# Reordered first loads, a smaller constant, and the second pair turned later, in a state-space kernel with a bilinear feed-forward layer

## The chip, the cores and the metric

The kernel runs on one core of one Trainium2 chip. The core has a matrix engine (TensorE, PE in the profile), three engines for elementwise work (VectorE or DVE, ScalarE or ACT, GpSimd or POOL), and a queue engine for transfers (SyncE or SP). SP, ScalarE and GpSimd can each issue transfers. The metric is the device time of one launch in microseconds, the median of three runs: before the change 125.71 us (125.55 to 125.74).

## The reference

Inputs are x (4 batches, 8 heads, 768 steps, 32 wide), a decay a per step, B and C (16 wide), and three weights of the feed-forward layer. The first stage is a chunked scan, the second a bilinear layer without a nonlinearity:

```python
for c in range(nc):                      # chunks of 32 steps, per batch and head
    cum = np.cumsum(log_a_chunk, axis=-1)
    L = np.exp(cum[..., :, None] - cum[..., None, :]) * causal
    y_intra = (C @ B.T * L) @ x
    y_inter = (C @ state) * np.exp(cum)[..., None]
    y[chunk] = y_intra + y_inter
    state = exp(sum(la)) * state + sum_j(B_j x_j exp(cum[-1] - cum_j))
x2 = y.transpose(0, 2, 1, 3).reshape(3072, 256)
out = ((x2 @ w_a) * (x2 @ w_b)) @ w_out  # w_a, w_b: 256 x 1536; w_out: 1536 x 256
```

## The kernel before

The kernel uses chunks of 128 steps (six blocks of the 768) and works on pairs of batches: pair 0 is block 0 of batches 0 and 1, pair 1 is block 0 of batches 2 and 3, pair 2 begins block 1, and so on to pair 11. For a pair it does the following.

- *Factors.* VectorE scans the products of a (`scan`, L236), takes reciprocals at the middle of a block (`over_mid`, L240), and scales a selector by them (`sel_over_mid`, L243). Eight small TensorE products for a block (`factors_mm`, L251) turn this into factors per step and head, in PSUM. ScalarE copies them to fC, and VectorE writes their reciprocals to fB.
- *Scaled B and C.* `scale_bc` (L310) multiplies B by fB into `bm` and C by fC into `cm`, for pair 0 on VectorE and for pairs 1, 2 and 3 on GpSimd.
- *Turns.* `transposes` (L326) turns bm and cm on TensorE (`turn`), copies the turned B twice into BT with two masks of rows (`copy_bt`), and copies the turned C into CT.
- *Scores, masks, outputs.* `scores` (L378) makes C times B in four PSUM banks SC, `mask` (L431) multiplies by the causal mask on VectorE, or by way of ScalarE on GpSimd, and `pv_u` (L440) multiplies by x, which `scale_x` (L297) has scaled to 16 bit. The result is evacuated into X2T.
- *Feed-forward.* `units_mm` (L637) and `unit` (L622 and L662) make products of X2T with Wa and Wb into banks `aps` and `bps`. ScalarE copies aps to `asb` (`evac_a`, L649), VectorE multiplies it with bps into hk (`times`, L654), and products with Wo give the output.

The order of the work is written out by hand: each engine executes its instructions in the order of the program, and waits at an instruction until its inputs are there. Every call of `bank` (L132) takes the next digit of the string BANKS as its PSUM bank, so the same string also decides which earlier work a TensorE group waits for.

The loads are issued in program order on their queues as well. SP loads a, parts of pair 0's inputs and the constants `ch` and `c32` (L182 to L194). ScalarE loads the other parts of pair 0 and then its activation table (L192). GpSimd loads pair 1's B and C, the first half of Wa in two pieces, the first piece of the first half of Wb, and pair 1's x (L219 to L227). It then scales pair 1's B and C, and only after that issues the second piece of Wb's first half and the second halves of Wa and Wb (L798 to L802). Later on its queue come pair 2's inputs and the two halves of Wo (L842 to L848). A transfer on GpSimd's queue also waits until the one eight places before it on that queue has landed, because eight completion counters are used in turn: the second half of Wo waits in this way for the second half of Wb. Pair 3's inputs go by SP and are held back by a dependency on the second half of Wb (L873, L874).

Before and between the early steps TensorE executes products on zeros (`warmup`, L229), whose results nobody reads.

Of the kernel before, what the change touches and what calls it, by code (L numbers as in the profile page):

```python
# [10 lines left out]
f32 = mybir.dt.float32  # L11
# [10 lines left out]
BANKS = (  # L22
    "0123120321032101320132013203120132013201321031230123012310321032130213021031203120321301"
    "2031203120312302130213021302103210321032103210321032103210231023102310231023102310231023"
    "102310231"
)
# [3 lines left out]
def kernel(  # L30
# [13 lines left out]
    nc = tc.nc  # L44
# [17 lines left out]
    bh = np.arange(BH)  # L62
    p32 = np.zeros((128, 128 + nb * NG), np.float32)
    p32[0:BH, 0:128] = (bh[:, None] % H) == (j[None, :] // N)
    for b in range(nb):
# [7 lines left out]
    const = ctx.enter_context(tc.tile_pool(name="const", bufs=1))  # L73
    c32 = const.tile([128, p32.shape[1]], f32, name="c32")
    ch = const.tile([128, H + 2], f32, name="ch")
# [69 lines left out]
    def load1(eng, p, which, bt, i0=0, n=64):  # L145
        blk, bp = divmod(p, NBP)
        if p >= P0:
            return eng.dma_start(
                by_token(pair_in[p][which])[:, bt],
                (B, C, x)[which][2 * bp + bt, :, blk * Q : (blk + 1) * Q, :].rearrange("h q n -> q h n"),  # L150
            )
        src = (B, C, x)[which][2 * bp + bt, :, blk * Q + 2 * i0 : blk * Q + 2 * i0 + 2 * n, :]
        return eng.dma_start(  # L153
            pair_in[p][which][64 * bt + i0 : 64 * bt + i0 + n].rearrange("i h r n -> i h (r n)"),
            src.rearrange("h (i r) n -> i h (r n)", r=2),
        )
# [19 lines left out]
    def load_wo(half):  # L176
        nc.gpsimd.dma_start(
            Wo[:, 6 * half : 6 * half + 6].rearrange("p (g kk) e -> p g (kk e)", kk=3),
            moe_w_out.rearrange("(g p kk) e -> p g (kk e)", p=128, kk=3)[:, 2 * half : 2 * half + 2],
        )  # L180

    nc.sync.dma_start(a_sb, a.rearrange("b h (k q) -> (b h) k q", q=Q))  # L182
    for p_ in range(3):
# [6 lines left out]
    load1(nc.scalar, 0, 1, 0, 32, 32)  # L190
    load1(nc.scalar, 0, 2, 1)
    nc.scalar.preload_act_table_set("natural_log_exp_and_others")  # L192
    load1(nc.sync, 0, 2, 0)
    nc.sync.dma_start(c32, p32_t.ap())  # L194
    nc.vector.memset(sel, 1.0)
# [4 lines left out]
    nc.vector.memset(hsx, 0.0)  # L200
    nc.vector.memset(causal_q, 1.0)
    nc.gpsimd.affine_select(
        out=sel,
# [10 lines left out]
    for bt in range(2):  # L214
# [3 lines left out]
        )  # L218
    load1(nc.gpsimd, 1, 0, 0)  # L219
    load1(nc.gpsimd, 1, 0, 1)  # L220
    load1(nc.gpsimd, 1, 1, 0)
    load1(nc.gpsimd, 1, 1, 1)
    load_w(Wa, 0, 0)
    load_w(Wa, 0, 1)
    load_w(Wb, 0, 0)
    for bt in range(2):
        load1(nc.gpsimd, 1, 2, bt)  # L227

# [97 lines left out]
    def transposes(p, ps=None, between=None, apart=False, tb2=None):  # L326
        s = st[p]
        if p >= P0:
            ps = [bank("tr").bitcast(f16)] * 2
            TB, TC = ps[0][:, 0:256], ps[0][:, 256:512]  # L330
            on_dve = False
        elif ps is None:
            ps = [SC[0], bank("tc") if p == 1 else SC[1]] if apart else None
            on_dve = apart
            TB, TC = (TT[:, 0:256], TT[:, 256:512]) if ps is None else [t_.bitcast(f16)[:, 0:256] for t_ in ps]
        else:
            on_dve = False
            TB, TC = [t_.bitcast(f16)[:, 0:256] for t_ in ps]
# [8 lines left out]
        def copy_bt(e):  # L347
            o_ = BT[:, e].rearrange("p r t i -> p (r t i)")
            if p == 0 and e:
                nc.vector.tensor_scalar(o_, tb2, par[:, e : e + 1], None, ALU.mult)  # L350
            else:
                b_.append(nc.scalar.activation(out=o_, in_=TB, func=AF.Copy, scale=par[:, e : e + 1]))  # L352

        turn(TB, s["bm"])
        if p == 1:
            copy_bt(0)
            copy_bt(1)
        if between:
            between()
        turn(TC, s["cm"])  # L360
        if p == 0:
            turn(tb2, s["bm"])
        if p != 1:
            copy_bt(0)
            copy_bt(1)
        if p >= P0:
# [4 lines left out]
            CT.rearrange("p t (i r) -> p r (t i)", r=2), TC.rearrange("p (r c) -> p r c", r=2)  # L371
        )
        if apart:
            for i_ in b_:
                tc.declare_no_dep(c_.ins, i_.ins.name, reason="reads of two banks")
# [401 lines left out]
    vr, fr = [t_.rearrange("p (r b h) -> p r b h", r=2, b=NBP) for t_ in (v, flat(fB, 0, 1))]  # L777
    nc.vector.reciprocal(fr[:, :, 0], vr[:, :, 0])
    warmup(2, SC[3])
# [5 lines left out]
    nc.vector.reciprocal(fr[:, :, 1], vr[:, :, 1])  # L785
    nc.scalar.copy(flat(fC, 0, 1), v)
    over_mid(1, 2)
    warmup(1, SC[3])
    warmup(2, SC[3], 128)
    scores(0)  # L790
    mask(product0(0, 0))
    mask(product0(0, 1))
    scale_x(0, nc.scalar)
    for e in range(2):
        mask(product0(1, e))
    warmup(2, tcp)
    warmup(2, tcp)
    scale_bc(1, 0, nc.gpsimd)  # L798
    scale_bc(1, 1, nc.gpsimd)
    load_w(Wb, 0, 1)  # L800
    load_w(Wa, 1)
    w1 = [load_w(Wb, 1)]  # L802
    sel_over_mid(1, 2, nc.gpsimd)
    nc.gpsimd.affine_select(
        out=causal_q, in_=causal_q, compare_op=ALU.is_ge, fill=0.0, base=0, pattern=[[1, Q]], channel_multiplier=-1
    )
    py = [bank("py0"), bank("py1")]
# [34 lines left out]
    for w in range(2):  # L842
        for bt in range(2):
            load1(nc.gpsimd, 2, w, bt)
    load_wo(0)
# [12 lines left out]
    nc.scalar.copy(maskbd, headm.unsqueeze(2).broadcast_to((128, H, D)))  # L858
# [242 lines left out]
```

## Time and profile before

| | us |
|---|---|
| median of three runs | 125.71 |
| the profiled execution | 125.44 |
| its span in the profile | 123.7 |
| TensorE busy (share of the span) | 117.1 (95%) |
| VectorE busy | 90.3 (73%) |
| ScalarE busy | 75.6 (61%) |
| GpSimd busy | 62.1 (50%) |

The profile is one execution. Its span is measured from the first to the last instruction that it shows, and the rest of its time lies around that. TensorE was granted its full clock in the whole span. A row of the timeline gives the start in us from the beginning of the span, the length in us, the engine, the line of the kernel, the operation, what it wrote and read, how many instructions are grouped, and in brackets how long the engine had been idle before and what ended that idle time. A row with SPq, ACTq or POOL and DMA_DIRECT2D is the issue of a transfer and not the transfer. A row of issues gives the size of one transfer and the median time from issue to landing.

### The profile page before, as it was taken

The page shows a single profiled execution, that of the slowest core. Times are in us where ns is not written, and L with a number is a line of the kernel's source. Part 1 is how long each engine was busy: PE and PEld are TensorE (multiplying, and loading weights), DVE is VectorE, ACT ScalarE, POOL GpSimd, SP SyncE. Part 2 cuts the span into 40 slices and gives each one's busy share as a digit, 9 for nine tenths or more (in the row PEclk, how much of TensorE's full clock was granted, in tenths as well). Part 3 has the DMA queues.
Part 4 walks back from the last instruction along what each step waited for, and adds up shares of the span by engine and source line. Part 5 has one row for each costly group of instructions (what it writes and reads, how often), then busy time and mean ns, then how long its engine had stood idle before and what let it go on. Part 6 is the DMA issues. An engine that isn't in the chain of part 4 may idle for free.

```text
span 123.7 us, 3723 instructions
## 1 busy us (share of the span) xinstructions
PE 117.1 (95%) x1467; PEld 80.7 (65%) x1467; DVE 90.3 (73%) x179; ACT 75.6 (61%) x158; POOL 62.1 (50%) x90
## 2 busy tenths in 40 slices
PE   5979799999999999999999999999999999999990
PEld 1436588889898798744467465757464775555890
DVE  3777898872995979799986988996889444747200
ACT  0447756827759856987669767457637746657220
POOL 6999996599392995097997970056000000000000
PEclk9999999999999999999999999999999999999999
DMA  3999999989999998689958921011101012010122
GB/s 65 160 184 205 156 213 212 168 154 91 99 117 129 89 123 109 70 109 102 89 171 182 276 56 45 5 42 45 42 0 48 0 42 87 5 42 0 42 85 85
DMA packets 56001, 12.21 MB, mean 99 GB/s; under 512 B 50640, under 2 KB 55504, under 8 KB 55984
## 3 DMA queue, kind: packets, MB, share of 16 engines
q1 hardware_dynamic: 51632, 7.42, 37.2%
q0 software_dynamic: 2352, 4.20, 18.8%
q10 hardware_dynamic: 2000, 0.36, 1.6%
q8 instruction: 11, 0.18, 0.6%
q14 instruction: 6, 0.05, 0.2%
HBM read 11.19 MB, written 3.15 MB: 116 GB/s over the span
## 4 chain that ended last, share of the span: by engine, by line
PE 79%; POOL 9%; DMA 7%; DVE 2%; issue 1%; ACT 0%; POOLq 0%
PE ops L730 17%; PE aps L705 17%; PE bps L705 16%; PE ops L673 9%; DMA Wb<-in_moe_w_b_dram 7%; PE aps L627 6%; PE bps L627 5%; PE SC L384 2%; PE SC L444 2%; PE tr L345 2%; POOL Wa L170 1%; POOL bn L153 1%; POOL cn L153 1%; POOL xn L153 1%; POOL cm L319 1%
## 5 line engine op out<-in xcount | busy, mean ns | idle before, releaser
L651 ACT COPY asb<-aps 128x512 f32<-128x512 f32 x72 | 42.0, 586 | 14.9 <-PE aps L705 10.3
L715 DVE TENSOR_TENSOR hkb<-bps,asb 128x512 f16<-128x512 f32 x48 | 32.4, 688 | 11.7 <-ACT asb L651 10.8
L705 PE MATMUL aps<-XB,Wa 128*128 128x512 f16 x96 | 28.6, 379 | 0.1
L705 PE MATMUL bps<-XB,Wb 128*128 128x512 f16 x96 | 28.5, 379 | 0.0
L730 PE MATMUL ops<-Wo,hkb 128*128 128x256 f16 (+1 forms) x204 | 22.8, 267 | 0.0
L730 PEld LDWEIGHTS <-hkb 128*128 128x128 f16 x204 | 18.5, 98 | 3.0
L438 DVE TENSOR_TENSOR t<-SC,causal_q 128x512 f16<-128x512 f32 x27 | 17.3, 681 | 2.2 <-PE SC L384 2.2
L658 DVE TENSOR_TENSOR hk<-bps,asb 128x512 f16<-128x512 f32 x24 | 15.7, 684 | 3.1 <-ACT asb L651 2.7
L705 PEld LDWEIGHTS <-Wb 128*128 128x128 f16 x96 | 9.9, 103 | 10.9
L705 PEld LDWEIGHTS <-Wa 128*128 128x128 f16 x96 | 9.7, 103 | 9.2 <-issue 0.3
L742 ACT ACTIVATE osb<-ops 128x256 f32<-128x256 f32 (+1 forms) x16 | 6.0, 376 | 12.7 <-PE ops L730 12.6
L627 PE MATMUL aps<-X2T,Wa 128*128 128x256 f16 x88 | 13.1, 273 | 0.0
L627 PE MATMUL bps<-X2T,Wb 128*128 128x256 f16 x84 | 12.5, 273 | 0.0
L308 POOL TENSOR_SCALAR x<-xn 128x512 f16<-128x512 f32 x8 | 11.9, 1489 | 0.8 <-DMA xn<-in_x_dram 0.2
L673 PE MATMUL ops<-Wo,hk 128*128 128x256 f16 x96 | 11.7, 273 | 0.0
L673 PEld LDWEIGHTS <-hk 128*128 128x128 f16 x96 | 9.0, 98 | 1.2
L627 PEld LDWEIGHTS <-Wa 128*128 128x128 f16 x88 | 8.8, 104 | 0.9 <-issue 0.2
L627 PEld LDWEIGHTS <-Wb 128*128 128x128 f16 x84 | 8.5, 103 | 0.6
L436 POOL TENSOR_TENSOR t<-tmp,causal_q 128x512 f16<-128x512 f32 x5 | 5.8, 1155 | 6.2 <-ACT tmp L435 6.1
L438 DVE TENSOR_TENSOR t<-SC,causal 128x512 f16<-128x512 f32 x13 | 8.2, 679 | 0.6 <-PE SC L399 0.6
L607 POOL TENSOR_TENSOR spair<-U,ch 128x128 f16<-128x128 f32 x8 | 3.1, 398 | 10.2 <-DVE U L591 10.2
L352 ACT ACTIVATE bt<-tr,ch 128x256 f16<-128x256 f16 x16 | 6.7, 472 | 0.5 <-PE tr L345 0.5
(105 smaller groups left out, 136.9 us busy)
## 6 DMA issues: line engine op xcount, KB each, us to landing
out_dram<-osb SPq DMA_DIRECT2D x23, 128.0 KB, 1.7
xn<-in_x_dram SPq DMA_DIRECT2D x5, 256.0 KB, 4.9
cn<-in_C_dram SPq DMA_DIRECT2D x8, 128.0 KB, 4.6
bn<-in_B_dram SPq DMA_DIRECT2D x8, 128.0 KB, 4.3
Wo<-in_moe_w_out_dram POOLq DMA_DIRECT2D x2, 384.0 KB, 6.2
xn<-in_x_dram POOLq DMA_DIRECT2D x3, 256.0 KB, 6.6
xn<-in_x_dram POOLq DMA_DIRECT2D x4, 128.0 KB, 5.5
xn<-in_x_dram SPq DMA_DIRECT2D x3, 128.0 KB, 4.9
```

The lines of the kernel that those rows point to most:

```text
L308: eng.tensor_scalar(xo, xi, XS, None, ALU.mult)
L352: b_.append(nc.scalar.activation(out=o_, in_=TB, func=AF.Copy, scale=par[:, e : e + 1]))
L436: nc.gpsimd.tensor_tensor(out=o_, in0=tmp, in1=c_, op=ALU.mult)
L438: nc.vector.tensor_tensor(out=o_, in0=i_, in1=c_, op=ALU.mult)
L627: nc.tensor.matmul(ps[:, kk * 2 * Q : (kk + 1) * 2 * Q], w_up(W, k, f), X2T[:, p, :, f], start=(f == 0), stop=(f == 1), skip_group_check=True,
L651: (nc.vector.tensor_copy if on_dve else nc.scalar.copy)(asb, a_ps)
L658: nc.vector.tensor_tensor(out=s["hk"][:, 2 * k2 : 2 * k2 + 2, :].rearrange("p k q -> p (k q)"), in0=b_ps, in1=asb, op=ALU.mult)
L673: nc.tensor.matmul(o_ps[:, 0:d_model], hk[:, k, bt * Q : (bt + 1) * Q], Wo[:, k, :], start=(k == 0), stop=(k == NK - 1), skip_group_check= ...
L705: nc.tensor.matmul(t_, w_up(W, k, f), XB[:, blk - P0 // NBP, f].rearrange("p t j q -> p (t j q)"), start=(f == 0), stop=(f == 1), skip_gro ...
L715: return lambda: nc.vector.tensor_tensor(out=s["hk"][:, k], in0=ps[1], in1=asb, op=ALU.mult)
L730: nc.tensor.matmul(o_ps[:, 0:w], hk[:, k, c * Q : (c + 1) * Q], Wo[:, k, cs], start=(k == 0), stop=(k == NK - 1), skip_group_check=True,)
L742: nc.scalar.activation(out=o_sb[:, 0:w], in_=o_ps[:, 0:w], func=AF.Copy, scale=1.0 / (YS * YS))
```

## The change

- GpSimd issues the second piece of Wb's first half right after one x transfer of pair 1, ahead of scaling pair 1's B and C.
- The other half of pair 1's x goes by SP. A dependency puts it behind the first reciprocal of factor 0.
- Pair 0's first half of x, one transfer on SP before, is split in two of 32 rows: one on SP, and one on ScalarE's queue ahead of the activation table.
- The constant c32 is loaded with 32 rows of 592 bytes instead of 128, and VectorE writes zeros to the tile first. The load moves behind the x transfer on SP.
- The factor products of block 1 move from behind the first Wb products to right behind pair 0's scores, into the bank that block 0's factors are in. One copy now takes both blocks' factors to fC. The scaling of the selector for block 1 moves from GpSimd to VectorE.
- Pair 1's turns: B is turned into a bank and C into SC[1] (before: SC[0] and a bank). The turn of C no longer comes after pair 0's second output products but before them. Of the two copies of the turned B, ScalarE makes the first and VectorE the second, after its copy of C.
- Pair 1's scores come behind six products with Wa. Three units' products with Wa are all issued early, and of the first products with Wb the last two come behind pair 1's outputs. ScalarE takes all four evacuations of pair 0's outputs.
- Pair 3's inputs are held back by the first half of Wo instead of the second half of Wb.
- BANKS is a new string for the new order.

```diff
-    p32 = np.zeros((128, 128 + nb * NG), np.float32)
+    p32 = np.zeros((BH, 128 + nb * NG), np.float32)
...
+    load1(nc.sync, 0, 2, 0, 0, 32)
+    load1(nc.scalar, 0, 2, 0, 32, 32)
     nc.scalar.preload_act_table_set("natural_log_exp_and_others")
-    load1(nc.sync, 0, 2, 0)
-    nc.sync.dma_start(c32, p32_t.ap())
...
+    nc.vector.memset(c32, 0.0)
+    x1 = load1(nc.sync, 1, 2, 0)
+    nc.sync.dma_start(c32[0:BH], p32_t.ap())
...
     load_w(Wb, 0, 0)
-    for bt in range(2):
-        load1(nc.gpsimd, 1, 2, bt)
+    load1(nc.gpsimd, 1, 2, 1)
+    load_w(Wb, 0, 1)
...
-            ps = [SC[0], bank("tc") if p == 1 else SC[1]] if apart else None
+            ps = [bank("tb") if p == 1 else SC[0], SC[1]] if apart else None
...
-            if p == 0 and e:
-                nc.vector.tensor_scalar(o_, tb2, par[:, e : e + 1], None, ALU.mult)
+            if p < 2 and e:
+                nc.vector.tensor_scalar(o_, tb2 if p == 0 else TB, par[:, e : e + 1], None, ALU.mult)
...
         turn(TB, s["bm"])
-        if p == 1:
-            copy_bt(0)
-            copy_bt(1)
...
         turn(TC, s["cm"])
         if p == 0:
             turn(tb2, s["bm"])
+        copy_bt(0)
         if p != 1:
-            copy_bt(0)
             copy_bt(1)
...
+        if p == 1:
+            copy_bt(1)
...
-    nc.vector.reciprocal(fr[:, :, 0], vr[:, :, 0])
+    f0 = nc.vector.reciprocal(fr[:, :, 0], vr[:, :, 0])
+    tc.add_manual_dep(x1.ins, f0.ins.name, AFTER, reason="x of pair 1 behind x of pair 0")
...
-    nc.scalar.copy(flat(fC, 0, 1), v)
     over_mid(1, 2)
+    sel_over_mid(1, 2, nc.vector)
...
     scores(0)
+    factors_mm(1, 2, fps0, 1)
     mask(product0(0, 0))
     mask(product0(0, 1))
+    scale_bc(1, 0, nc.gpsimd)
+    nc.scalar.copy(flat(fC, 0, 2), fps0[:, 0:64])
     scale_x(0, nc.scalar)
...
-    warmup(2, tcp)
-    warmup(2, tcp)
-    scale_bc(1, 0, nc.gpsimd)
     scale_bc(1, 1, nc.gpsimd)
-    load_w(Wb, 0, 1)
     load_w(Wa, 1)
-    w1 = [load_w(Wb, 1)]
-    sel_over_mid(1, 2, nc.gpsimd)
+    load_w(Wb, 1)
...
+    warmup(4, tb2)
...
-    def second():
-        pv_u(0, 1, py, True)
-        for bt in range(2):
-            evac0(1, bt, (nc.scalar, nc.vector)[bt], py)
-
-    transposes(1, between=second, apart=True)
+    transposes(1, apart=True)
+    pv_u(0, 1, py, True)
+    for bt in range(2):
+        evac0(1, bt, nc.scalar, py)
     scan(3, 5)
-    aps = [bank("aps") for _ in range(2)]
-    units_mm(0, (0, 1), Wa, aps, 0, range(4))
-    units_mm(0, (0, 1), Wa, aps, 1, range(2))
+    aps = [bank("aps") for _ in range(3)]
+    units_mm(0, range(3), Wa, aps, 0, range(6))
+    scores(1)
+    mask(product(1, 3), by_pool=True)
+    units_mm(0, range(3), Wa, aps, 1, range(6))
     asb = [evac_a(aps[0])]
-    scores(1)
-    units_mm(0, (0, 1), Wa, aps, 1, range(2, 4))
-    mask(product(1, 3), by_pool=True)
-    aps.append(unit_mm(0, 2, Wa))
-    asb.append(evac_a(aps[1]))
     scale_x(1, nc.scalar)
-    asb.append(evac_a(aps[2]))
+    asb += [evac_a(aps[1]), evac_a(aps[2])]
...
+    tiles(3)
     bps = [bank("bps") for _ in range(3)]
-    units_mm(0, range(3), Wb, bps, 0, range(6))
-    tiles(3)
+    units_mm(0, range(3), Wb, bps, 0, range(4))
     pv(1, DS=(0, SC[:2]))
     ds_mm(0, 64, SC[:2])
+    units_mm(0, range(3), Wb, bps, 0, range(4, 6))
     units_mm(0, range(3), Wb, bps, 1, range(6))
-    fps = bank("fps")
-    factors_mm(1, 2, fps)
-    nc.scalar.copy(flat(fC, 1, 2), fps[:, 0:32])
...
-    tc.add_manual_dep(b3[0].ins, w1[0].ins.name, AFTER, reason="weights ahead of pair 3's inputs")
+    tc.add_manual_dep(b3[0].ins, wo0.ins.name, AFTER, reason="weights ahead of pair 3's inputs")
```

More of the change, by code (lines that the diff above doesn't have):

```diff
@@ L22 @@
 BANKS = (
-    "0123120321032101320132013203120132013201321031230123012310321032130213021031203120321301"
-    "2031203120312302130213021302103210321032103210321032103210231023102310231023102310231023"
-    "102310231"
+    "0123130213021302312031203102312031203120321023012301230210321032013201321023102310320123"
+    "1023102310230132013201320132103210321032103210321032103213021302130213021302130213021302"
+    "13021302"
 )
@@ L62 @@
     bh = np.arange(BH)
-    p32 = np.zeros((128, 128 + nb * NG), np.float32)
-    p32[0:BH, 0:128] = (bh[:, None] % H) == (j[None, :] // N)
+    p32 = np.zeros((BH, 128 + nb * NG), np.float32)
+    p32[:, 0:128] = (bh[:, None] % H) == (j[None, :] // N)
     for b in range(nb):
@@ L73 @@
     const = ctx.enter_context(tc.tile_pool(name="const", bufs=1))
-    c32 = const.tile([128, p32.shape[1]], f32, name="c32")
+    c32 = const.tile([128, 128 + nb * NG], f32, name="c32")
     ch = const.tile([128, H + 2], f32, name="ch")
@@ L176, in load_wo @@
     def load_wo(half):
-        nc.gpsimd.dma_start(
+        return nc.gpsimd.dma_start(
             Wo[:, 6 * half : 6 * half + 6].rearrange("p (g kk) e -> p g (kk e)", kk=3),
@@ L218 @@
         )
[L219 to L222, printed above, removed]
+    for w in range(2):
+        for bt in range(2):
+            load1(nc.gpsimd, 1, w, bt)
     load_w(Wa, 0, 0)
@@ L790 @@
     scores(0)
+    factors_mm(1, 2, fps0, 1)
     mask(product0(0, 0))
     mask(product0(0, 1))
+    scale_bc(1, 0, nc.gpsimd)
+    nc.scalar.copy(flat(fC, 0, 2), fps0[:, 0:64])
     scale_x(0, nc.scalar)
-    for e in range(2):
-        mask(product0(1, e))
-    warmup(2, tcp)
-    warmup(2, tcp)
-    scale_bc(1, 0, nc.gpsimd)
+    mask(product0(1, 0))
+    mask(product0(1, 1))
     scale_bc(1, 1, nc.gpsimd)
-    load_w(Wb, 0, 1)
     load_w(Wa, 1)
-    w1 = [load_w(Wb, 1)]
-    sel_over_mid(1, 2, nc.gpsimd)
+    load_w(Wb, 1)
     nc.gpsimd.affine_select(
@@ L810 @@
         evac0(0, bt, nc.scalar, py)
-    def second():
-        pv_u(0, 1, py, True)
-        for bt in range(2):
-            evac0(1, bt, (nc.scalar, nc.vector)[bt], py)
-    transposes(1, between=second, apart=True)
-    scan(3, 5)
-    aps = [bank("aps") for _ in range(2)]
-    units_mm(0, (0, 1), Wa, aps, 0, range(4))
-    units_mm(0, (0, 1), Wa, aps, 1, range(2))
-    asb = [evac_a(aps[0])]
-    scores(1)
-    units_mm(0, (0, 1), Wa, aps, 1, range(2, 4))
-    mask(product(1, 3), by_pool=True)
-    aps.append(unit_mm(0, 2, Wa))
-    asb.append(evac_a(aps[1]))
+    transposes(1, apart=True)
+    pv_u(0, 1, py, True)
+    for bt in range(2):
+        evac0(1, bt, nc.scalar, py)
+    scan(3, 5)
+    aps = [bank("aps") for _ in range(3)]
[3 more added lines that the diff above has]
+    units_mm(0, range(3), Wa, aps, 1, range(6))
+    asb = [evac_a(aps[0])]
     scale_x(1, nc.scalar)
-    asb.append(evac_a(aps[2]))
+    asb += [evac_a(aps[1]), evac_a(aps[2])]
     for m in range(3):
@@ L844 @@
             load1(nc.gpsimd, 2, w, bt)
-    load_wo(0)
+    wo0 = load_wo(0)
     for bt in range(2):
```

## The prediction

> **What bounds the kernel now.** I read the page's shares first, then the chain of waits in order of time, then a table of windows, then the timeline of the first 22 us.
>
> ```profile
> span 123.7 us, 3723 instructions
> ...
> PE 117.1 (95%) x1467; PEld 80.7 (65%) x1467; DVE 90.3 (73%) x179; ACT 75.6 (61%) x158; POOL 62.1 (50%) x90
> ```
> ```profile
> 21.70:123.70 102.00, 98.93 (x1186) 68.24 (x1186) 73.75 (x133) 64.08 (x134) 43.06 (x56) 1.00 0.50 83
> ```
> TensorE is the bound, but not from the start. The second fence is the table of windows (length, then TensorE's busy time first; the last two columns are DMA share and GB/s). From 21.7 on TensorE is busy for 98.93 of 102.00 us, so what is won or lost before that passes to the end. What decides when the dense part begins is in the chain (start, length, what):
>
> ```profile
> 11.16 8.30 DMA Wb<-in_moe_w_b_dram
> 19.46 0.28 issue
> 19.74 0.67 POOL Wo L177
> ...
> 21.09 0.62 POOL cm L319
> 21.71 0.05 issue
> 21.76 0.29 PE SC L345 x2
> ```
> The second half of Wb is issued at 11.16 and lands at 19.46. GpSimd, waiting to issue the second half of Wo, goes on only then, and behind that stand pair 2's bm and cm; TensorE turns cm at 21.76. The timeline gives the price:
>
> ```profile
> 19.74 0.72 POOL L177 DMA_DIRECT2D Wo<-in_moe_w_out_dram  x1 [1.10 <-DMA Wb<-in_moe_w_b_dram]
> 21.75 0.11 PEld L345 LDWEIGHTS <-cm 128*128 128x128 f16 x2 [0.25 <-POOL cm L319]
> ```
> TensorE waits only 0.25 us here, so a gain of its own before this point is worth nothing unless that landing moves too; it would only lengthen the wait. The end therefore moves with the landing of Wb's second half, up to a cap that TensorE's own path sets.
>
> **The change, part by part: the DMA stream.** GpSimd's transfers go out in issue order, and the list of issues and the windows show the stream they make:
>
> ```profile
> 7.03 1.49 POOL L153 DMA_DIRECT2D xn<-in_x_dram  x2
> 9.86 0.61 POOL L170 DMA_DIRECT2D Wb<-in_moe_w_b_dram  x1
> ```
> ```profile
> c<-p SPq DMA_DIRECT2D x1, 74.0 KB, 4.5
> ```
> ```profile
> 5.50:7.50 2.00, 1.66 (x44) 1.08 (x44) 1.06 (x6) 0.99 (x3) 2.00 (x4) 1.00 1.13 191
> 7.50:8.50 1.00, 0.82 (x4) 0.20 (x2) 1.00 (x2) 0.13 (x1) 1.00 (x2) 1.00 1.07 152
> 8.50:10.50 2.00, 1.26 (x38) 0.89 (x39) 1.48 (x4) 1.57 (x6) 1.84 (x5) 1.00 1.16 201
> 10.50:11.75 1.25, 1.18 (x40) 0.70 (x38) 1.25 (x4) 0.55 (x3) 1.25 (x2) 1.00 1.23 250
> 11.75:12.50 0.75, 0.75 (x15) 0.71 (x8) 0.57 (x1) 0.75 (x3) 0.66 (x3) 1.00 0.92 132
> ```
> An x transfer of pair 1 is 128 KB: 64 rows of 8 heads, 64 values of 4 bytes. The engines are taken (share about 1, the column before GB/s) from 5.5 to 11.75 us, and both queues share them, so a later landing goes by the work queued ahead of it.
> (a) Wb's second piece is now issued behind one x transfer, about 7.75 instead of 9.86. From 11.75 to 12.50 the stream falls to 132 GB/s, at 0.92 share; its queue held nothing issued between 8.52 and 9.86. At the 201 GB/s of 8.5 to 10.5 the hole is 0.75 x (1 - 132/201) = 0.26 us; at 250, 0.35. I take 0.26 gained; the ends are 0.35 gained and 0, if the dip has another cause.
> (b) Half of pair 1's x (128 KB) leaves GpSimd's queue, where it cost 128/250 = 0.51 us, and goes by SP, issued about 5.3 (after the reciprocal of factor 0) and moving beside the first weights. There it costs 128/191 = 0.67 us, the rate while SP's and ScalarE's loads of small pieces flowed, or 128/152 = 0.84. From 7.5 to 8.5 the stream runs 49 GB/s under its later rate, room for 0.24 us; I let it fill half. Net 0.67 - 0.51 - 0.12 = 0.04 us lost; ends 0.51 gained (all beside other work) and 0.33 lost.
> (c) The constant shrinks from 74 to 18.5 KB: 55.5/191 = 0.29 us. Most of it moved before the weights, and time freed there has nothing to fill it: I take 0.09 gained, ends 0 and 0.29.
> Sum: 0.26 + 0.09 - 0.04 = 0.31 us earlier; Wb's second half lands at 19.15, and pair 2's cm is done 0.31 sooner.
>
> A rule speaks against (b): the Trainium skill (DMA: Bandwidth & Descriptors, section "Issuing engines are not separate DMA queues") says that transfers begun by several engines share the same 16 DMA engines and interleave, so that another issuer only saves issue time. The share of about 1 in these windows agrees. By that rule there is no room to fill, (b) is 0.67 - 0.51 = 0.16 us lost, and the sum is 0.19, inside the first rival.
>
> **TensorE's own path, which sets the cap.**
>
> ```profile
> 2.96 0.41 DVE L238 TENSOR_TENSOR_SCAN Pr<-a_sb,zero 32x128 f32<-32x128 f32 x1 [1.02 <-DMA a_sb<-in_a_dram]
> 2.93 0.61 ACTq L153 DMA_DIRECT2D xn<-in_x_dram  x1
> 3.57 1.28 ACT L192 ACT_TABLE_LOAD   x1 [3.57 <-issue]
> 6.06 0.47 ACT L352 ACTIVATE bt<-tb,ch 128x256 f16<-128x256 f16 x1 [1.21 <-PE tb L345]
> 7.49 2.48 DVE L438 TENSOR_TENSOR t<-SC,causal 128x512 f16<-128x512 f32 x4 [0.45 <-PE SC L399]
> 8.37 0.63 ACT L306 ACTIVATE x<-xn 128x512 f16<-128x512 f32 x1 [1.12 <-DMA xn<-in_x_dram]
> 9.05 0.30 PE L459 MATMUL py<-t,x 64*32 64x128 f16 x16 [0.73 <-ACT x L306]
> 9.30 0.62 POOL L319 TENSOR_TENSOR cm<-cn,fC 128x256 f16<-128x256 f32 x1
> 13.22 0.63 ACT L306 ACTIVATE x<-xn 128x512 f16<-128x512 f32 x1 [0.19 <-DMA xn<-in_x_dram]
> 13.90 0.42 PE L459 MATMUL SC<-t,x 64*32 64x128 f16 x32 [0.44 <-ACT x L306]
> 14.43 0.60 ACT L522 ACTIVATE X2T<-SC 128x512 f16<-128x512 f32 x1
> 15.59 0.41 PE L260 MATMUL fps<-selr,Pr 32*64 32x16 f32 x8
> 16.01 0.62 PE L627 MATMUL aps<-X2T,Wa 128*128 128x256 f16 x4
> ```
> ```profile
> L651 ACT COPY asb<-aps 128x512 f32<-128x512 f32 x72 | 42.0, 586 | 14.9 <-PE aps L705 10.3
> ```
> Free edits first. The zeroing of c32 goes into VectorE's 1.02 us wait for a. ScalarE issues 32 rows of pair 0's x before its table load, which ends near 5.5 instead of 4.85, ahead of its first work at 6.06; without that cover it costs the 0.61 of one issue. The scaling of the selector moves from GpSimd to VectorE, into the 0.45 us before the first mask; the masks slip by what does not fit there, which I put at nothing. The eight factor products (0.41 us) go from 15.59 to behind pair 0's scores, into the 0.73 us in which TensorE waits for x; the longer fC copy then sits ahead of ScalarE's x, inside its 1.12 us wait. The four fillers stay four and end nearer to the output products. Pair 0's x comes on two queues and may land 0.3 earlier, but the second mask ends at 7.49 + 2.48/2 = 8.73, so the first output products start near 8.8, not 9.05.
> Pair 1 is turned later: its cm turn is now queued ahead of the second output products and waits for GpSimd's cm (9.30 to 9.92 before; one issue of Wb stands ahead of it now instead of one of x, about as long, so 9.7 to 10.1 is its end after). The last mask ends at 7.49 + 2.48 = 9.97 anyway, so that queueing costs 0 to 0.2. Of pair 1's B, VectorE now makes one copy and ScalarE one, and ScalarE takes the evacuation that VectorE had, so neither gets longer. Scores of pair 1 come behind six Wa products instead of a wait, some 0.4 sooner. That gain stops at x: pair 1's second x transfer is still behind Wb's first piece, so I put its landing at 13.2 as now (0.3 either way), and ScalarE now has two copies of a (0.59 each, the last row) between x and X2T. X2T then ends about 13.2 + 0.63 + 2 x 0.59 + 0.60 = 15.6, against 15.03. The factor products no longer stand behind it, so Wa on pair 1 starts near 15.65 instead of 16.01: 0.35 sooner, ends 0 and 0.6. The new bank order puts other releases ahead of those products; I count it at nothing, since the copies and products that release them end by 15.6 too. At the other end one copy's 0.59 more would bring TensorE to pair 2's cm at 21.74: no gain and no loss. As counted, TensorE would come to pair 2's cm at 21.51 - 0.35 = 21.15; the gate is at 21.76 - 0.31 = 21.45. The gate wins by 0.3, and the cap on any gain is 0.25 + 0.35 = 0.6 us.
>
> **Pair 3's loads** wait on Wo's first half instead of Wb's last:
>
> ```profile
> Wo<-in_moe_w_out_dram POOLq DMA_DIRECT2D x1, 384.0 KB, 5.9
> ```
> ```profile
> 16.49 0.77 POOL L177 DMA_DIRECT2D Wo<-in_moe_w_out_dram  x1
> 19.48 1.29 SPq L153 DMA_DIRECT2D bn<-in_B_dram  x2
> 27.77 0.62 POOL L319 TENSOR_TENSOR cm<-cn,fC 128x256 f16<-128x256 f32 x1
> 30.29 0.28 PE L345 MATMUL SC<-ident,cm 128*128 128x128 f16 x2
> ```
> Wo's first half lands at 16.49 + 5.9 = 22.4, so every load on SP's queue starts up to 2.9 us later. Pair 3's cm ends at 28.39 and is turned at 30.29: 1.9 us of cover, so the price is 0, or 1.0 if all of the delay came through. I take 0: the stream is full in between, so a later issue finds the work ahead of it done.
>
> **The sum.** The profiled execution took 125.44 us, its span 123.7 and 1.7 around it; the median of the runs is 125.71, 0.27 above. 125.71 - 0.31 = 125.4 us.
>
> **The rivals.** (1) Hidden anyway: the stream is conserved, (a) only moves the hole, and Wb's last half lands within 0.25 of 19.46, gating cm again: 125.5 to 125.9, centre 125.7. For it: the share near 1 everywhere. Against it: the fall to 132 GB/s at 0.92 share, which is time that nobody used. (2) Slower: SP's half of x, in small pieces beside the weights, delays them by 0.33 us, and (a) and (c) bring nothing: Wb lands at 19.8, 126.05 us. It decides as soon as the SP transfer costs the weights over 0.25 more than (a), (c) and the freed 0.51 give back. For it: 152 GB/s from 7.5 to 8.5, when small pieces still flowed. (3) The loads of pair 3 come through: up to 1.0 late, 126.4 us; against it, the cover of 1.9. (4) The landing moves by 0.6 or more and TensorE's path sets the time: 125.1.
>
> **How the numbers follow.** A measurement of this kernel can tell about 0.2%, 0.25 us. The forecast (gain of 0.25 to 0.5) has 0.33, rival (4) 0.13, rival (1) 0.25, rival (2) 0.22, rival (3) 0.07: faster 0.46, within 0.2% 0.25, slower 0.29. The likeliest case's own range is 125.2 to 125.45; the range of 125.0 to 126.1 holds (4), (1) and (2) and leaves out (3) and the tails.
>
> **What would show it.** Wb's second piece issued near 7.8 and no fall at 12 us; the wait at Wo's second half ending near 19.15; pair 2's cm ended near 21.4 and TensorE waiting there about 0.3 us; eight factor products near 7.4 and none near 15.6; Wa on pair 1 near 15.65; SP's first bn of pair 3 near 22. Wrong it would be made by a landing of Wb at 19.4 or later, or by a TensorE wait for pair 3's cm or bm near 30 us.

## The result and the profile after

The changed kernel takes 125.14 us (median of five runs, 125.03 to 125.27), the kernel before 125.74 on the same chip (125.55 to 125.99): a ratio of 0.995, interval 0.9935 to 0.9965, or 0.60 us. The profiled execution took 125.15 us with a span of 123.4, against 125.44 and 123.7. So the two profiles show 0.3 us, and the medians twice that; below comes what the profiles show, and what of the rest stays open. Here and below the ratios with their intervals leave out the executions that took over 1.5% longer than the shortest of their kernel (one to three of twelve in three of the runs, one of six in the last), while the medians are of all.

The page of the changed kernel, its span and its shares:

```profile
span 123.4 us, 3725 instructions
...
PE 117.8 (95%) x1467; PEld 80.7 (65%) x1467; DVE 90.6 (73%) x181; ACT 75.5 (61%) x157; POOL 61.4 (50%) x88
```

The shares are what they were. Its windows, in the columns of the prediction (the last two are DMA share and GB/s), and then two windows of the kernel before that the prediction did not show:

```profile
7.50:8.50 1.00, 1.00 (x18) 0.63 (x12) 0.83 (x2) 0.51 (x2) 0.94 (x3) 1.00 1.05 155
...
10.50:11.75 1.25, 1.20 (x40) 0.74 (x38) 0.87 (x4) 0.45 (x2) 0.95 (x2) 1.00 1.14 253
11.75:12.50 0.75, 0.75 (x22) 0.54 (x6) 0.58 (x1) 0.52 (x2) 0.00 (x0) 1.00 1.25 230
12.50:16.00 3.50, 2.83 (x82) 2.16 (x81) 2.83 (x9) 2.93 (x7) 3.35 (x5) 1.00 1.11 198
16.00:19.50 3.50, 3.50 (x32) 3.04 (x31) 3.18 (x7) 2.12 (x5) 3.39 (x5) 1.00 0.88 157
21.40:123.40 102.00, 99.08 (x1189) 68.25 (x1186) 74.07 (x133) 64.41 (x134) 42.57 (x55) 1.00 0.49 83
```
```profile
12.50:16.00 3.50, 2.78 (x85) 1.87 (x82) 3.02 (x10) 2.23 (x5) 3.38 (x5) 1.00 1.03 156
16.00:19.50 3.50, 3.50 (x34) 3.33 (x34) 2.95 (x6) 2.48 (x7) 2.64 (x4) 1.00 1.08 211
```

The fall near 12 us is gone (230 GB/s where 132 stood), and the next 3.5 us move 198 GB/s where 156 stood. The work of the first part comes in sooner, and between 16 and 19.5 us the stream now has slack (0.88). The dense part, 102 us from 21.4 on, is as long and as full as it was.

The timeline of the changed kernel, beside the row of the second half of Wb in the list of issues (size, then us from issue to landing):

```profile
8.43 0.62 POOL L321 TENSOR_TENSOR bm<-bn,fB 128x256 f16<-128x256 f32 x1
10.33 0.73 POOL L170 DMA_DIRECT2D Wb<-in_moe_w_b_dram  x1
15.44 1.89 DVE L659 TENSOR_TENSOR hk<-bps,asb 128x512 f16<-128x512 f32 x3 [0.53 <-PE bps L641]
15.61 0.60 PE L628 MATMUL aps<-X2T,Wa 128*128 128x256 f16 x4
16.18 0.60 PE L628 MATMUL bps<-X2T,Wb 128*128 128x256 f16 x4
16.78 0.60 PE L628 MATMUL aps<-X2T,Wa 128*128 128x256 f16 x4
18.61 0.78 POOL L177 DMA_DIRECT2D Wo<-in_moe_w_out_dram  x1
20.19 0.61 POOL L321 TENSOR_TENSOR cm<-cn,fC 128x256 f16<-128x256 f32 x1
21.29 0.28 PE L347 MATMUL SC<-ident,bm 128*128 128x128 f16 x2
21.40 0.28 PE L347 MATMUL SC<-ident,cm 128*128 128x128 f16 x2
```
```profile
Wb<-in_moe_w_b_dram POOLq DMA_DIRECT2D x1, 384.0 KB, 7.8
```

Wb's second half is issued at 10.33 and lands at 10.33 + 7.8 = 18.1, where it landed at 19.46. GpSimd issues Wo's second half at 18.61 with no wait, pair 2's cm is done at 20.8, and TensorE turns it at 21.40 without waiting; before, it turned at 21.76 after a wait. The chain of waits of the changed kernel no longer runs through that landing. In this execution it runs through the landing of pair 1's x and then through TensorE's own products:

```profile
7.03 6.33 DMA xn<-in_x_dram
...
15.77 0.44 PE aps L628 x4
16.21 0.58 PE bps L628 x4
16.78 0.60 PE aps L628 x4
...
21.45 0.24 PE SC L347 x4
```

This is the rival in which the landing moves by 0.6 or more and TensorE's own path sets the time.

### The profile page after: what moved, and what is told of

Its sections match the earlier page's. It is cut to its first block, busy times and chain, and to the rows that moved or that the text cites. A ratio compares the mean times of both kernels' runs of the same rounds, so it can differ in the third digit from the quotient of the medians.

```text
span 123.4 us, 3725 instructions
## 1 busy us (share of the span) xinstructions
PE 117.8 (95%) x1467; PEld 80.7 (65%) x1467; DVE 90.6 (73%) x181; ACT 75.5 (61%) x157; POOL 61.4 (50%) x88
## 4 chain that ended last, share of the span: by engine, by line
PE 84%; DMA 5%; POOL 4%; ACT 2%; DVE 2%; issue 1%
PE ops L731 17%; PE aps L706 17%; PE bps L706 16%; PE ops L674 9%; PE bps L628 7%; PE aps L628 7%; DMA xn<-in_x_dram 5%; PE SC L385 2%; PE SC L445 2%; PE tr L347 2%; POOL bn L153 1%; POOL cn L153 1%; POOL Wa L170 1%; PE SC L460 1%; PE SC L535 1%; PE bps L641 1%
## 5 line engine op out<-in xcount | busy, mean ns | idle before, releaser
L731 PEld LDWEIGHTS <-hkb 128*128 128x128 f16 x204 | 18.5, 98 | 2.9
L659 DVE TENSOR_TENSOR hk<-bps,asb 128x512 f16<-128x512 f32 x24 | 15.5, 683 | 2.8 <-ACT asb L652 2.1
L628 PE MATMUL aps<-X2T,Wa 128*128 128x256 f16 x84 | 12.5, 273 | 0.0
```

The source lines that it names most:

```text
L628: nc.tensor.matmul(ps[:, kk * 2 * Q : (kk + 1) * 2 * Q], w_up(W, k, f), X2T[:, p, :, f], start=(f == 0), stop=(f == 1), skip_group_check=True,
L659: nc.vector.tensor_tensor(out=s["hk"][:, 2 * k2 : 2 * k2 + 2, :].rearrange("p k q -> p (k q)"), in0=b_ps, in1=asb, op=ALU.mult)
L731: nc.tensor.matmul(o_ps[:, 0:w], hk[:, k, c * Q : (c + 1) * Q], Wo[:, k, cs], start=(k == 0), stop=(k == NK - 1), skip_group_check=True,)
```

## The experiments

All are compared with the kernel before on their own chip. One kernel's executions scatter: the 35 of the kernel before in the first set went from 125.17 to 127.03. Differences of 0.2 us between two kernels of a set are therefore not settled by a set. Each run has a profile of one execution, so the rows show that execution and not the median.

**The changed kernel again.**

> The changed kernel once more, unaltered, timed in the same rounds as the runs beside it. Theory G (the landing of Wb's second half set the end before, and TensorE's own path sets it now) and theory T (the gain is TensorE's own: factor products and turns moved, the landing is incidental) both expect about 125.1 us, 0.6 under the kernel before.

125.17 against 125.64, ratio 0.9952 (0.9925 to 0.9978). The gain of 0.5 us stands. This execution's timeline differs from the first:

```profile
13.29 0.62 PE L641 MATMUL bps<-X2T,Wb 128*128 128x256 f16 x4 [0.63 <-DMA Wb<-in_moe_w_b_dram]
18.95 0.72 POOL L177 DMA_DIRECT2D Wo<-in_moe_w_out_dram  x1 [0.46 <-DMA Wb<-in_moe_w_b_dram]
21.46 0.28 PE L347 MATMUL SC<-ident,cm 128*128 128x128 f16 x2
29.43 0.62 POOL L321 TENSOR_TENSOR cm<-cn,fC 128x256 f16<-128x256 f32 x1 [1.24 <-DMA cn<-in_C_dram]
30.11 0.28 PE L347 MATMUL SC<-ident,cm 128*128 128x128 f16 x2
```

Wb's second half lands at about 18.7 here (10.33 and 8.3), so GpSimd does wait, 0.46 us, and the turn of pair 2's C still comes within 0.06 us of the first execution's. TensorE waits 0.63 us for Wb's first piece.

**The loads alone**: the kernel before with all changed transfers and the old order of work.

```
-    load1(nc.sync, 0, 2, 0)
-    nc.sync.dma_start(c32, p32_t.ap())
+    load1(nc.sync, 0, 2, 0, 0, 32)
+    load1(nc.scalar, 0, 2, 0, 32, 32)
...
+    x1 = load1(nc.sync, 1, 2, 0)
+    nc.sync.dma_start(c32[0:BH], p32_t.ap())
...
+    load1(nc.gpsimd, 1, 2, 1)
+    load_w(Wb, 0, 1)
...
-    load_w(Wb, 0, 1)
     load_w(Wa, 1)
```

> The kernel before with the changed loads alone (Wb's second piece ahead of GpSimd's scaling, half of pair 1's x and a 32-row constant by SP, pair 0's x in two parts, pair 3's inputs behind Wo's first half); the order of the compute as before. Theory G: Wb's second half lands near 18.1 instead of 19.46, GpSimd no longer waits, TensorE comes to pair 2's turn of C at about 21.5 and doesn't wait: 0.25 us gained, 125.5 us. Theory T: nothing gained, 125.7 us.

125.61 against 125.64, ratio 1.0002 (0.9966 to 1.0038), an interval too wide to read; a second set (below) has it again. Its profiled execution, at 125.16 us, was as short as the changed kernel's. In its timeline the gate has moved as in the changed kernel, pair 2's cm is ready 0.5 us ahead of its turn, and the turn comes as early as there:

```profile
18.97 0.72 POOL L177 DMA_DIRECT2D Wo<-in_moe_w_out_dram  x1 [0.15 <-issue]
20.29 0.63 POOL L322 TENSOR_TENSOR cm<-cn,fC 128x256 f16<-128x256 f32 x1
21.39 0.28 PE L348 MATMUL SC<-ident,cm 128*128 128x128 f16 x2
```

**The order of work alone**: the changed kernel with the transfers of the kernel before, the same edits the other way round.

> The changed order of the compute alone, with the loads as before. Theory G: GpSimd still waits for Wb's second half until 19.5, pair 2's C is turned at 21.7 to 21.8 as before, and TensorE only waits longer there (0.4 to 0.6 us instead of 0.25): no gain, 125.6 to 125.8 us. Theory T: nearly the whole gain, 125.1 to 125.3 us.

125.47, ratio 0.9977 (0.9947 to 1.0007). Its timeline has the old landing back:

```profile
15.40 0.84 PE L638 MATMUL bps<-X2T,Wb 128*128 128x256 f16 x6 [0.33 <-DMA Wb<-in_moe_w_b_dram]
19.75 0.72 POOL L177 DMA_DIRECT2D Wo<-in_moe_w_out_dram  x1 [0.93 <-DMA Wb<-in_moe_w_b_dram]
21.86 0.27 PE L344 MATMUL SC<-ident,cm 128*128 128x128 f16 x2
```

With the old transfers, the new order meets a second piece of Wb that is not there yet (0.33 us), GpSimd waits 0.93 for the second half, and the turn comes at 21.86, 0.1 later than before. In this execution the new order gained nothing. The median's 0.17 us lies inside the interval and between the two expectations, so the time alone decides for neither; beside the changed kernel on this chip it is 0.30 slower.

**The gate moved**: the kernel before with Wo's second half issued behind pair 2's scaling, so that GpSimd's wait for Wb stands ahead of nothing that TensorE needs soon.

```
         load1(nc.gpsimd, 2, 2, bt)
-    load_wo(1)
...
     scale_bc(2, 1, nc.gpsimd)
+    load_wo(1)
```

> The kernel before with one edit: the second half of Wo is issued behind the scaling of pair 2's B and C instead of ahead of it, so that the wait for Wb's second half no longer stands ahead of them. Theory G: bm and cm then wait only for their own inputs, which landed at 20.2 and 20.9; cm ends near 21.55 instead of 21.71: 0.1 to 0.15 us gained, 125.6 us. Theory T: nothing, 125.7 us.

125.49, ratio 0.9988 (0.996 to 1.0016). The timeline:

```profile
20.14 0.61 POOL L319 TENSOR_TENSOR bm<-bn,fB 128x256 f16<-128x256 f32 x1 [0.94 <-DMA bn<-in_B_dram]
20.72 0.61 POOL L319 TENSOR_TENSOR cm<-cn,fC 128x256 f16<-128x256 f32 x1
21.79 0.28 PE L345 MATMUL SC<-ident,cm 128*128 128x128 f16 x2
```

The wait at Wo is gone, and 0.94 us of it comes back as a wait for pair 2's B, whose transfer stands behind the same half of Wb in GpSimd's queue. The cm is ready 0.37 us sooner than before (21.33 against 21.71), but TensorE came to it no sooner, at 21.79. Its own path was late in this execution: a piece of Wa landed at 11.56, pair 1's scores came at 11.93 (11.36 before), and the first products with Wa on pair 1 at 16.28 (16.01 before). So freeing cm did not shorten this execution, and what it is worth with TensorE's path in its former place isn't shown. Wb's second half landed at 18.9 here (issued 11.12, 7.8 us), 0.5 us sooner than in the profile of the kernel before, with the same transfers queued ahead of it: the landing moves by that much with no edit to the stream ahead of it.

**Wb's second piece back behind the scaling** (the changed kernel without part (a)):

```
-    load_w(Wb, 0, 1)
...
     scale_bc(1, 1, nc.gpsimd)
+    load_w(Wb, 0, 1)
     load_w(Wa, 1)
```

> The changed kernel with one edit undone: Wb's second piece is issued behind the scaling of pair 1's B and C again. Theory H (the fall of the stream near 12 us was a hole left by the late issue): the fall to about 130 GB/s between 11.75 and 12.5 returns, the piece lands near 15.0 to 15.3, Wb's second half 0.3 to 0.8 us later than 18.1, TensorE waits for the piece ahead of its second products with Wb, 0.2 to 0.4 us lost: 125.4 to 125.5 us. Rival S (the engines are full, so only the order of the landings changes): no fall, the second half of Wb still near 18.1, 125.1 to 125.2 us.

125.43 against 125.51, ratio 0.9996 (0.9969 to 1.0023), with executions from 124.95 to 127.05. A window of its profiled execution, which took 124.95:

```profile
11.75:12.50 0.75, 0.75 (x23) 0.69 (x8) 0.58 (x1) 0.53 (x2) 0.00 (x0) 1.00 1.02 166
```

Part of the fall near 12 us is back (166 GB/s), so the piece's place does fill that hole. But Wb's second half lands at 18.55 (issued 10.35, 8.2 us), inside the 18.1 to 18.7 of the changed kernel. So most of the earlier landing does not hang on the hole. TensorE does not wait for the moved piece, and it turns pair 2's C at 21.19, 0.21 sooner than in the changed kernel, since pair 1's x was in use at 12.93 and not at 13.38. Whether (a) is worth anything in time, this run doesn't tell: the median of all twelve executions says that it carries most of the gain, that of the ten shorter ones (125.33) that it carries a part, and the profiled execution that it carries none.

**Pair 1's x on GpSimd again** (without part (b)):

```
-    x1 = load1(nc.sync, 1, 2, 0)
...
-    load1(nc.gpsimd, 1, 2, 1)
+    for bt in range(2):
+        load1(nc.gpsimd, 1, 2, bt)
     load_w(Wb, 0, 1)
```

> The changed kernel with both x transfers of pair 1 on GpSimd's queue again, ahead of Wb's second piece. If SP's transfer is nearly free (moved beside other work), the second piece and the second half of Wb land about 128/250 = 0.5 us later and x no sooner: 0.2 to 0.4 us lost, 125.4 to 125.5 us. If it costs the weights what it frees, as the prediction counted (0.04 us net), nothing moves: 125.1 to 125.2 us. If it costs more than it frees, Wa's and Wb's first pieces land earlier and TensorE's wait of 0.3 us for Wb's first piece goes: 124.9 to 125.1 us.

125.47 against 125.51, ratio 1.0004 (0.9987 to 1.0021), eight of its twelve executions between 125.44 and 125.50: the gain is gone. The time is that of the first case expected, but not by its way, a later landing. What its timeline shows instead:

```profile
7.03 1.49 POOL L153 DMA_DIRECT2D xn<-in_x_dram  x2
9.15 0.62 POOL L321 TENSOR_TENSOR bm<-bn,fB 128x256 f16<-128x256 f32 x1
9.83 0.29 PE L347 MATMUL tb<-ident,bm 128*128 128x128 f16 x2 [0.53 <-POOL bm L321]
10.41 0.28 PE L347 MATMUL SC<-ident,cm 128*128 128x128 f16 x2 [0.29 <-POOL cm L321]
21.63 0.28 PE L347 MATMUL SC<-ident,cm 128*128 128x128 f16 x2
```

The second x costs GpSimd 0.7 us of issuing ahead of pair 1's scaling, whose bm starts at 9.15 where the changed kernel has 8.43. TensorE waits 0.53 and 0.29 us for bm and cm. The chain of waits of this execution runs from that bm and cm through pair 1's masks to pair 1's outputs, which start at 14.30 (14.06 in the changed kernel), and TensorE comes to pair 2's C at 21.63, 0.23 later than there. Wb's second half is issued 0.7 later too (11.04), and lands at 18.5 all the same. So with Wb's piece ahead of the scaling too, (b) pays by GpSimd's time, and not in the stream. (In the kernel before, two issues of x stood ahead of the scaling and Wb's piece behind it; in the changed kernel one of each stands ahead, here all three.)

**Pair 3's loads behind Wb's last piece again.**

```
-    load_w(Wb, 1)
+    w1 = load_w(Wb, 1)
...
-    tc.add_manual_dep(b3[0].ins, wo0.ins.name, AFTER, ...)
+    tc.add_manual_dep(b3[0].ins, w1.ins.name, AFTER, ...)
```

> The changed kernel with pair 3's inputs held back by Wb's second half again instead of Wo's first half, so SP starts them near 18 to 19 us instead of 22.8. If the cover counted in the prediction holds, the end stays: 125.1 to 125.2 us, with GpSimd's waits for pair 3's B and C (0.5 us, in the second profile 0.6 and 1.2) gone. If those waits reach TensorE in most executions: 0.1 to 0.3 us gained, 124.9 to 125.0 us. If the earlier issue takes the engines from pair 2's inputs and Wo: 0.1 to 0.3 lost, and a wait for pair 2's B or C shows.

125.15 against 125.51, ratio 0.9991 (0.9973 to 1.0008): by the median most of the gain is there, by the ratio little of it, so no price of this wait can be read. Pair 3's waits disappear and nothing follows from it. In this execution Wb's half landed at 19.0, and pair 2's cm was late again:

```profile
19.34 0.72 POOL L177 DMA_DIRECT2D Wo<-in_moe_w_out_dram  x1 [0.84 <-DMA Wb<-in_moe_w_b_dram]
21.34 0.11 PEld L347 LDWEIGHTS <-cm 128*128 128x128 f16 x2 [0.22 <-POOL cm L321]
```

That row shows how near the two gates now lie: with a landing at 19.0 it is GpSimd's, at 18.7 TensorE's own. (The chain of waits of this execution names the landing of pair 2's C at 19.93, just ahead of the end of that issue; the two can't be told apart here.)

**The order of pair 0's products**: four products of factor 1 ahead of the last two of factor 0, so that the banks of bps fill, and VectorE starts on them, sooner.

```
-    units_mm(0, range(3), Wb, bps, 0, range(4, 6))
-    units_mm(0, range(3), Wb, bps, 1, range(6))
+    units_mm(0, range(3), Wb, bps, 1, range(4))
+    units_mm(0, range(3), Wb, bps, 0, range(4, 6))
+    units_mm(0, range(3), Wb, bps, 1, range(4, 6))
```

> The changed kernel with the last two of the first products with Wb put behind the first four of the second products, so that the first bank is complete 0.2 us sooner for VectorE. If VectorE's release of banks is what holds TensorE on pair 1 now (TensorE begins its second group with Wa at 16.78, right after VectorE's second product), that group starts near 16.55 and up to 0.2 us is gained: 124.95 us. If the next wait takes it back (pair 2's scores behind VectorE's copy), pair 2's scores stay near 23.04: 125.1 to 125.2 us.

124.87 against 125.51, ratio 0.9949 (0.9934 to 0.9965). Timeline:

```profile
15.33 0.60 PE L628 MATMUL aps<-X2T,Wa 128*128 128x256 f16 x4
15.77 0.60 PE L628 MATMUL bps<-X2T,Wb 128*128 128x256 f16 x4
16.20 0.60 PE L628 MATMUL aps<-X2T,Wa 128*128 128x256 f16 x4
...
19.80 0.61 POOL L321 TENSOR_TENSOR bm<-bn,fB 128x256 f16<-128x256 f32 x1 [0.59 <-DMA bn<-in_B_dram]
```

Groups of four products now follow each other every 0.44 us; in the changed kernel the same three stood at 15.61, 16.18 and 16.78, held 0.13 and 0.16 us more. That was VectorE's release of the banks: its first products for pair 0 now begin at 14.84 and not at 15.44. TensorE reaches pair 2's B at 20.71, 0.58 sooner than in the changed kernel. The holds are 0.29 of that; 0.28 is there already at the first of the three groups (15.33, not 15.61), with pair 1's x in use at 12.90 and not at 13.38. Then GpSimd's cm, late through the landing of pair 2's B, lets it turn C only at 21.05. Nine of the twelve executions took 124.58 to 125.11 us and three 126.51 to 128.22.

A second set put four kernels on one chip, each with twelve executions, against 125.71 for the kernel before.

> The changed kernel again, beside the two below on one chip. If its gain is the one measured at first, the ratio is 0.995 (0.5 to 0.7 us); if the first figure was half luck, 0.9975. TensorE waits at pair 2's C turn for nothing, or for less than 0.1 us, at about 21.4 us.

The changed kernel: 125.19, ratio 0.9963 (0.9938 to 0.9987). Pair 2's C turned at 21.38, no wait. In this execution the chain runs through pair 1's masks, which end at 14.00, and not through the landing of its x.

> The kernel before with the changed loads alone, again, since its first comparison was too wide to read. Theory (the landing of Wb's second half carries the gain, and the changed order of work adds little): 0.3 to 0.5 us faster than before, within 0.2 of the changed kernel on this chip. Rival (both are needed; the order of work is what lets TensorE use the earlier landing): within 0.2 us of before, and 0.4 or more slower than the changed kernel.

The loads alone: 125.75, ratio 1.0007 (0.9972 to 1.0042). The rival of this expectation holds: the loads alone are within 0.04 us of before and 0.56 slower than the changed kernel. In its profiled execution (125.34 us) the turn came at 21.57, with no wait for cm. Four of its twelve executions took 126.48 to 126.96, where none of the changed kernel's took over 125.82; no profile shows one of these.

> The changed kernel with four products of bps on factor 1 moved ahead of the last two of factor 0, now beside the changed kernel on one chip. Theory (VectorE's release of the banks holds TensorE from 16.1 to 16.8 in the changed kernel): TensorE comes to pair 2's B turn 0.4 to 0.6 us earlier (20.7 to 20.9) and then waits about 0.2 for GpSimd's C, so 0.2 to 0.4 us faster than the changed kernel. Rival (that hold is made up by the wait for GpSimd): within 0.15 us of it.

The other order of products: 125.13, ratio 0.9965 (0.9935 to 0.9995), 0.06 from the changed kernel. Its timeline shows what takes the gain back:

```profile
20.95 0.62 POOL L321 TENSOR_TENSOR cm<-cn,fC 128x256 f16<-128x256 f32 x1 [0.74 <-DMA cn<-in_C_dram]
21.63 0.28 PE L347 MATMUL SC<-ident,cm 128*128 128x128 f16 x2 [0.39 <-POOL cm L321]
```

The holds are gone here too, and TensorE was at B at 20.97, 0.3 sooner than in the changed kernel; but pair 2's C had not landed. What the order of products frees, the landing can take back.

> The kernel with that order of products, and B and C of pair 2 issued by SP's queue once Wb's second piece has landed (about 14), where GpSimd issued them at 13.6 and 15.0 behind both second halves of the weights. Theory (in that kernel the landing of pair 2's B, behind the second half of Wb in GpSimd's queue, gates the C turn again): GpSimd's B of pair 2 no longer waits 0.6 us, its C is done by 20.4, the turn of C at 20.9 or before with no wait, 0.1 to 0.3 us faster than the kernel it is made from. Rival (the stream is full, so what goes first only pushes the other back): Wb's second half lands at 20 or later, its use by TensorE or GpSimd's wait for it at Wo moves back, 0.2 to 0.8 us slower than the kernel it is made from.

The edit to the kernel with that order:

```
+    b2 = [load1(nc.sync, 2, 0, bt) for bt in range(2)]
+    tc.add_manual_dep(b2[0].ins, w01.ins.name, AFTER, ...)
+    for bt in range(2):
+        load1(nc.sync, 2, 1, bt)
-    for w in range(2):
-        for bt in range(2):
-            load1(nc.gpsimd, 2, w, bt)
     wo0 = load_wo(0)
```

131.48, ratio 1.0433 (1.0385 to 1.0481): 6.3 us slower than the kernel it was made from, and not by either theory. From its timeline and its chain of waits:

```profile
13.53 1.28 SPq L153 DMA_DIRECT2D bn<-in_B_dram  x2
24.05 0.61 POOL L321 TENSOR_TENSOR bm<-bn,fB 128x256 f16<-128x256 f32 x1 [7.50 <-DMA bn<-in_B_dram]
24.72 0.37 PE L347 MATMUL SC<-ident,bm 128*128 128x128 f16 x2 [3.74 <-POOL bm L321]
25.66 1.06 PE L628 MATMUL aps<-X2T,Wa 128*128 128x256 f16 x4
```
```profile
15.53 9.14 DMA cn<-in_C_dram
```

Wb's second half is not pushed back (issued 10.46, 7.7 us: 18.2). It is the small loads that come late. Issued by SP at 13.5 to 15.5, they land between 21.5 and 24.7, while GpSimd, with four issues fewer, had put both halves of Wo and pair 2's x into its queue by 16.6. In GpSimd's queue B and C stood ahead of Wo, and a 64 KB load took 4.3 us; on a queue of their own they move beside Wo, and the last took 9.1. That it is Wo that holds them up is the nearest account; no run kept Wo back to show it.

The late loads bring the turn of C to 25.47, 3.84 later than in the profile of the kernel that this one was made from (21.63), where the two profiled executions lie 5.4 apart. Most of the rest is TensorE's clock: after the gap of 3.74 us without a product its granted clock is 0.51 from 24.72 to 28.20, where it is 1.00 before and after, and a group of four products takes 1.06 us and not 0.60. By estimate half the clock over these 3.5 us costs some 1.7 us.

## Why the prediction was right, and where it was not

It said 125.4 us, faster by 0.31. Measured: 125.14, faster by 0.60 at first, and by 0.47 and 0.52 in the two repetitions.

- **What bounds the kernel: right for the kernel before; that the change needs both of its halves fits, and is not shown.** The prediction put GpSimd's gate at 21.76 and TensorE's own path 0.25 before it. Loads alone can then gain 0.25 at most, and the order of work alone nothing. Measured: 0.03 us gained and 0.04 lost for the loads alone (intervals that allow 0.43 and 0.35 gained), 0.17 gained for the order alone (interval from 0.67 gained to 0.09 lost), and 0.5 for both. The profiles don't show the need for both: the turn of C comes at 21.39 and 21.57 with the loads, nearly as early as with both (21.38 to 21.46), and at 21.86 with the order. So what the loads alone lack beside both lies in executions without a profile.
- **The sum of the stream, 0.31 us: the term that was mis-sized.** Wb's second half was to land at 19.15; it landed at 18.1, 18.7 and 18.7 in three executions, 0.8 to 1.3 us earlier than before. (Some of this can be scatter: with the transfers of the kernel before it landed at 19.46, 19.5 and 18.9.) So the gate did not stay ahead of TensorE's path by 0.3, it fell behind it, and the case that came is rival (4), which named the condition (0.6 or more) and the time (125.1).
- **That the forecast case's time was near is in part luck.** The turn of C was to come at 21.45 by the gate and came at 21.40 by TensorE's own path. Two misses meet there: the landing came 0.4 to 1.0 sooner than counted, and TensorE's path 0.25 later (21.40, not 21.15).
- **(a), 0.26 us from the hole near 12 us: the hole was read rightly, its worth was not.** Issued at 7.74 (7.75 forecast), it fills the hole; with the piece moved back, the hole returns in part and the landing is 18.55.
- **(b), 0.04 lost in the stream: the wrong account.** Undone, the landing is 18.5, inside the scatter of the changed kernel's, so the stream showed neither loss nor gain. But 0.7 us of GpSimd's issuing comes back ahead of pair 1's scaling, TensorE waits 0.82 us in all near 10 us, and the gain over the kernel before is gone. The prediction had counted "one issue of Wb stands ahead of it now instead of one of x, about as long", and did not ask what a second one would cost. The rule of the Trainium skill (DMA: Bandwidth & Descriptors, "Issuing engines are not separate DMA queues") that another issuer only saves issue time agrees with this: the issue time, 0.7 us of GpSimd's, is what undoing (b) showed.
- **(c) was not tried alone.** The landing stays near 18.5 when (a) or (b) is undone, and is 18.9 to 19.5 with all old transfers, so what moves it is (c), the two queues for pair 0's x, or several parts each of which is enough. This stays open, the more so as the landing moves by 0.6 us between executions of one kernel.
- **TensorE's path: right until 15.6, then a term at nothing that was 0.3.** Wa on pair 1 at 15.61 (15.65 forecast), factor products at 7.53, pair 1's x landed at 13.36 (13.2). The step that failed is the bank order, counted "at nothing, since the copies and products that release them end by 15.6 too": VectorE's three products begin at 15.44 and run 1.89 us, and hold TensorE 0.13 + 0.16 us. The 0.40 won at 15.61 are 0.13 at 18.66 (18.79 before). The other order of products removes these holds. One gain on this path did not come: pair 1's scores were to come some 0.4 sooner and came at 11.42 (11.36 before), so the masks behind them end at 13.8 to 14.0, about when pair 1's x is ready.
- **Pair 3's loads at nothing: right in the price, not in the cover.** SP's first issue came at 22.84 (22 forecast), GpSimd waited 1.24 for C in one execution, and its cm ended at 30.05, 0.06 us ahead of the turn at 30.11: there the 1.9 us were used up, no more.
- **Not foreseen**: TensorE's wait for Wb's first piece, 0.63 us in the second execution, beside transfers that now go out sooner. ScalarE got pair 1's x only at 13.44 in that execution, and TensorE would have waited for that in any case.
- **What stays open**: the profiles show 0.3 us of a gain that the medians put at 0.5 to 0.6. The profiled execution of the kernel before was 0.27 under its median, that of the changed kernel at its median. A kernel gated by a landing passes each late landing on, one with slack there does not; that would fit, and was not shown. Three of the four long executions of the loads alone had a mean granted clock of 0.984 to 0.986, all others of that run 1.000. In the kernel with pair 2's loads on SP a mean of 0.987 goes with a long wait of TensorE; whether these three had one isn't known.

The best time is that of the kernel with the other order of products, ratio 0.9949 and 0.9965 to the kernel before; beside the changed kernel on one chip it was 0.06 us apart, which is no difference.

## What to carry to other kernels

Where two paths meet within some tenths of a us, give each its arrival time and price an edit against the gap: an edit on one path is worth the gap at most, and two that gain nothing alone can gain together. An issue is work of the engine that makes it: moving a 0.7 us issue out from ahead of a scaling was worth more here than anything it did to the stream. And a load that is wanted early was better placed ahead in the busy queue here (4.3 us for 64 KB) than on another queue beside it (up to 9.7).

## What the runs showed of the hardware that was not expected

- A DMA share near 1 says little of the rate: at shares of 1.05 to 1.25 the changed kernel's windows moved from 155 to 253 GB/s.
- Small loads on SP's queue beside a filled GpSimd queue took 8.0 to 9.7 us for 64 KB, where the same loads in GpSimd's queue took 4.3 (the median of four for B).
- After 3.74 us without a product TensorE's granted clock was 0.51 for 3.5 us, in the kernel with pair 2's loads on SP.
- With the transfers of one kernel nearly the same, the landing hardly depends on the issue: Wb's second half, issued at 10.33 or at 11.04, landed at 18.1 to 18.7 and at 18.5. Issued at 11.12 to 11.20 in the old stream, it landed at 18.9 to 19.5.
- The same kernel's landing moved by 0.6 us between executions, and its times by 0.8 (124.87 to 125.65 in twelve).
